# Pooled attention with a SoLU feed-forward: later key loads, transposes on TensorE in its transpose form, and the first tile's scores half by half

## The chip, the cores and the metric

The kernel runs on one core of a Trainium2 chip. A core has TensorE (matrix products into PSUM), VectorE, ScalarE, GpSimd and SyncE, each with an instruction queue of its own; DMAs are issued from the queues of SyncE and ScalarE and share sixteen DMA engines. The metric is the device time of one execution in microseconds (us), as the median of several runs.

## The reference

Two stages in a row. The attention pools `kv` over 4x4 patches (768 keys for each of 4 batches, keys and values the same), and the feed-forward is a SoLU with a layer norm inside:

```python
kv_pool = kv.reshape(B, H // r, r, W // r, r, C).mean(axis=(2, 4))
k = v = kv_pool.reshape(B, -1, C) @ w_sr
s = scale * (q @ k.transpose(0, 2, 1))          # 12288 queries x 768 keys, 4 batches
a = exp(s - s.max(-1)); a /= a.sum(-1) + 1e-09
x = a @ v
h = x @ w_in                                     # 128 -> 1024
solu = h * softmax(h)
ln = (solu - mean) / sqrt(var + 1e-06) * g_ln
out = ln @ w_out                                 # 1024 -> 128
```

All data are float32; the queries are eight times as large as the attention's setup draws them. The output has 49152 rows of 128.

## The kernel before

The 49152 query rows are 384 tiles of 128 rows, four tiles to a group, 96 tiles to a batch. Each product of two float32 operands is made of three products of high and low halves (fp16, or fp32r for the scores of batch 0, where `wide` holds).

One loop runs over slots 0 to 383 (L1081 to L1147). A slot works on several tiles at once, each in another stage: scores and their exponential for tile `slot`, values for an earlier group, h, its exponential and u for tile `slot - 10`, and the output product o for tile `slot - 13`. The order of the calls in the loop is the order of the instructions on every engine, since it is written by hand (`manual_schedule`, L888).

For one tile: `scores_pe` (L580) makes the scores s in PSUM, 128x768, as two halves of 384 columns with three products each; `scores_exp` (L600) takes the maximum on VectorE (nm), the exponential on ScalarE in place and a scaled copy to fp16 (phl, L614); `scores_split` (L617) makes the low half and has SyncE's queue transpose both through a DMA (pT). `values` (L630) accumulates xa on TensorE, `hidden_pe` makes h, `hidden_max`, `hidden_exp` and `hidden_u` make u on VectorE and ScalarE, `hidden_high` and `hidden_low` split u on GpSimd (uhl), `hidden_turn` (L778) transposes it through a DMA on SyncE's queue (uT, four buffers), `hidden_var` (L801) squares u on ScalarE, and `final_pe` (L816) makes o with 24 products of 128 columns.

SyncE's queue holds, per group of four slots, eight of these transposing DMAs, one query load (qf, 256 KB, in the fourth slot) and one output store (out, 256 KB, in the second).

The keys of the next batch are prepared while the current one runs. `kv_plan` (L502) gives each step a slot: sixteen loads of 384 KB (`kv_load`, L226, on ScalarE's queue), additions on GpSimd (`kv_add`), and from slot 70 the steps of `key_steps` (L1039): keys, their squares and halves, and for the batches 1 and 2 the values, in slots 82, 83 and 86 (`kv_vp` on TensorE, `kv_vo` on ScalarE), then their high and low halves on GpSimd. `kv_vp` multiplies two 128x128 blocks of the keys by a diagonal matrix `dg`, which transposes and scales them; it writes to the part of a scores tile in PSUM that the scores leave free. Batch 0's keys are made ahead of the loop, half by half (L941 to L960), with the first two tiles' scores behind them (L1079, L1080). The last tile's u is transposed on TensorE, by a product with the identity (`hidden_turn_pe`, L782), and copied out by ScalarE and VectorE (room).

In the loop the key loads of a slot stand at its end, behind everything else:

```python
        for st in todo:
            if st[0].func is kv_add:
                for f in st:
                    f()
            elif len(st) == 1:
                st[0]()
```

Of the kernel before, what the change touches and what calls it, by code (L numbers as in the profile page):

```python
# [31 lines left out]
GT = 4  # L32
# [29 lines left out]
FIT_AT = 302  # L62

SOON = {0: (), 1: (8, 8), 2: (8, 8), 3: (27, 33), 4: (39, 45), 5: (51, 54)}
LATE = {6: (12, 16, 18), 7: (16, 20, 22)}


@with_exitstack
def kernel(
# [15 lines left out]
    nc = tc.nc  # L85
# [64 lines left out]
    state = {}  # L150
# [133 lines left out]
        nc.vector.tensor_scalar(kq[:, 1:2], kq[:, 2:3], SCALE, None, op0=ALU.mult)  # L284

    def kv_rescale():
        small(state["dg", 0], state["dg", 0], state["kq", 0][:, 2:3])
        nc.gpsimd.tensor_tensor(
            root, state["sv", 0][:, 0:1], state["kq", 0][:, 2:3], op=ALU.mult
        )  # L290
# [51 lines left out]
    def small(dst, src, first, second=1.0):  # L342
        nc.gpsimd.tensor_scalar(dst, src, first, second, op0=ALU.mult, op1=ALU.mult)
# [88 lines left out]
    def in_pairs(name, b, c):  # L432
        return state[name, b][:, c * 256 : c * 256 + 256].rearrange("p (j k) -> p j k", j=2)
# [9 lines left out]

    def kv_vp(b, c):
        for j in range(2):
            nc.tensor.matmul(
                state["free"][:, j, :],
                in_pairs("kT", b, c)[:, j, :],
                state["dg", b],
                start=True,  # L450
                stop=True,
            )

    def kv_vo(b, c):
        nc.scalar.copy(in_pairs("vf", b, c), state["free"])

    def kv_v_high(b, half):
        nc.gpsimd.tensor_scalar(
# [43 lines left out]
    def kv_plan(b):  # L502


        for pos in range(RR):


            if b == 1 and pos in SOON:
                for half, slot in enumerate(SOON[pos]):
                    yield slot, [partial(kv_add, b, half, pos)]  # L510
                continue
            slot = 6 * pos - (28 if b == 1 else 30)
            load, *adds = (slot // GT * GT, slot + 3, slot + 5)
            if b == 1 and pos in LATE:
                load, *adds = LATE[pos]
            yield load, [partial(kv_load, b, pos)]
            if pos:
                for half, add in enumerate(adds):
                    yield add, [partial(kv_add, b, half, pos)]
        for slot, half, *fs in key_steps(b):  # L520
            yield slot, [partial(f, b, half) for f in fs]
# [18 lines left out]
    def wide(g):  # L540
        return g < GPB or g >= NG

    def q_scale(g):
        if wide(g) or NG <= g:
            return
        qf = state["qf", g // QL][:, (g % QL) * 512 : (g % QL + 1) * 512]
        nc.gpsimd.tensor_scalar(
            qf, qf, state["kq", g // GPB][:, 1:2], 1.0, op0=ALU.mult, op1=ALU.mult
        )
# [30 lines left out]
    def scores_pe(t):  # L580
        g, j = divmod(t, GT)
        b = t // TPB
        qh, ql = state["q", g]
        names = ("kwh", "kwl") if wide(g) else ("kh", "kl")
        kh, kl = (state[n, b] for n in names)
        tokens = in_tiles if wide(g) else by_tile
        s = ps_r.tile([P, 2, 512], F32, tag="r", name=f"s_{t}")
        for n, (lh, rh) in enumerate(((qh, kh), (qh, kl), (ql, kh))):
            for half in range(2):
                nc.tensor.matmul(  # L590
                    s[:, half, :384],
                    tokens(lh)[:, j, :],
                    rh[:, half * 384 : (half + 1) * 384],
                    start=n == 0,
                    stop=n == 2,
                )
        state["s", t] = s[:, :, :384]
        state["free"] = s[:, :, 384:]

# [182 lines left out]
    def hidden_turn_pe(t):  # L782

        u, _ = state["u", t]
        pt = ps_r.tile([P, DFF], F32, tag="r", name=f"ut_{t}")
        for c in range(NFC):
            cs = slice(c * P, (c + 1) * P)
            nc.tensor.matmul(pt[:, cs], u[:, cs], ident, start=True, stop=True)
        state["ut", t] = pt.rearrange("p (c d) -> p c d", c=NFC)

    def hidden_turned_high(t):
# [9 lines left out]
    def hidden_var(t):  # L801
        g, j = divmod(t, GT)
        u, su = state.pop(("u", t))

        junk = wrk.tile([P, DFF], BF16, tag="junk", name=f"junk_{t}", bufs=1)
        nc.scalar.activation(  # L806
            junk,
            u,
            AF.Square,
            scale=-float(DFF),  # L810
            bias=su,
            accum_out=state["v3", g][:, j : j + 1],
        )
# [54 lines left out]
    root = fit[:, B - 1 : B]  # L868
    ident = const.tile([P, P], F32, name="ident")
# [39 lines left out]
    for _ in range(WARM):  # L909
# [4 lines left out]
            start=True,  # L914
            stop=True,
# [123 lines left out]
    def key_steps(b):  # L1039
        steps = [  # L1040
            (70, 0, kv_kp, kv_ko), (71, 1, kv_kp, kv_ko), (74, 2, kv_kp, kv_ko),
            (72, 0, kv_sq), (75, 1, kv_sq),
            (77, 0, kv_kh), (79, 1, kv_kh),
            (78, 0, kv_kl), (80, 1, kv_kl),
        ]
        if b < B - 1:
            return steps + [
                (82, 0, kv_vp, kv_vo), (83, 1, kv_vp, kv_vo), (86, 2, kv_vp, kv_vo),
                (84, 0, kv_v_high), (85, 0, kv_v_low), (87, 1, kv_v_high), (88, 1, kv_v_low),
            ]  # L1050
        return steps + [
            (82, 0, kv_v_scale), (84, 1, kv_v_scale),
            (83, 0, kv_vt_high), (86, 1, kv_vt_high),
            (86, 0, kv_vt_low), (88, 1, kv_vt_low),
            (90, 0, kv_v_turn),
        ]
# [3 lines left out]
    def at(t, fn, *args):  # L1060
        if 0 <= t < NT:
            fn(t, *args)

    def at_last(t, fn, *args):

        if 0 <= t < NT and t % GT == GT - 1:
            fn(t // GT, *args)

    def at_soon(t, fn):

        at_last(t, fn) if t >= GT else fn(0) if t == GT - 2 else None
# [9 lines left out]
    for slot in range(NT):  # L1081
        i = slot - LH
        av, qtr = divmod(slot - LAV - GT + 1, GT)
        tb, ti = divmod(slot, TPB)
        if ti == 12 and tb + 1 < B:
            kv_alloc(tb + 1)
        qs = GT if slot < 2 * GT else 2 * GT + 1 if slot < 3 * GT else 3 * GT + QSP
        todo = plan.pop(slot, [])
        at(slot, scores_exp)
        for f in held:  # L1090
            f()
        held = []
        if slot <= LH:
            at(slot - 1, scores_split)
        at(i - 1, hidden_u)
        at_last(slot - XSP - 1, values_split)
        if slot < 9:
            for f in fill.pop(slot, []):
                f()
        if 0 <= av < NG:  # L1100
            values(av, qtr, 0)
        if slot != 8:
            at(slot + 2 if slot < 8 else slot + 1, scores_pe)
        at_soon(slot - NORM, values_norm)
        at_last(slot - FSC, final_scale)
        at(i - 1, hidden_high)
        at(i - 1, hidden_low)
        at_last(slot - FSC, final_root)
        if slot < NT and 0 < qs < slot and (slot - 1 - qs) % GT == 0:
            q_low(slot // GT + 1)  # L1110
        if slot < NT and 0 < qs <= slot + 1 and (slot + 1 - qs) % GT == 0:
            q_scale((slot + 1) // GT + 1)
        if slot < NT - 1:
            at(i - 1, hidden_var)
        at(i, hidden_max)
        at(i, hidden_exp)
        if slot == NT - 1:
            hidden_var(i - 1)
        for f in fill.get(slot, []):
            f()  # L1120
        pairs = [st for st in todo if len(st) > 1 and st[0].func is not kv_add]
        for st in pairs:
            st[0]()
        if 0 <= av < NG:
            values(av, qtr, 1)
        for st in pairs:
            held += st[1:]
        if slot >= LH:
            at(slot, scores_split)
        at_soon(slot - NORM, values_recip)  # L1130
        at_soon(slot - NORM, values_recip_u)
        at(i + 1, hidden_pe)
        if slot < NT - 1:
            at(slot - LO, final_pe)
        at(i - 1, hidden_turn)
        if slot % GT == GT - 1:
            q_load(slot // GT + 3)
        at_last(slot - LO - 1, final_out)
        at_last(slot - XSP, values_out)
        for st in todo:  # L1140
            if st[0].func is kv_add:
                for f in st:
                    f()
            elif len(st) == 1:
                st[0]()
        if slot < NT and 0 < qs <= slot and (slot - qs) % GT == 0:
            q_split(slot // GT + 1)  # L1147
# [144 lines left out]
    n = nc.values_load(count[0:1, 0:1], min_val=0, max_val=P)  # L1292
# [37 lines left out]
```

## Time and profile before

| what | us |
|---|---|
| median of 3 runs | 1836.55 |
| lowest and highest | 1835.77, 1844.36 |
| the profiled execution's own time | 1841.4 |
| its span, first to last instruction | 1839.5 |
| TensorE busy in the span | 1818.2 |
| VectorE, ScalarE, GpSimd busy | 1768.4, 1749.2, 1665.6 |

TensorE's clock was granted at 0.999 of full speed over the span. The busy time of an engine is the time in which it ran an instruction; waiting, branching and the issue of DMAs are not counted. Matmuls are pipelined, so TensorE's busy time has products that overlap. A group of four tiles takes between 18 and 20 us, and nearly all groups look alike, so what a change does is read from the few stretches that differ.

### The profile page before, as it was taken

The numbers are of one execution on the slowest core, as the hardware profiler recorded it, in microseconds if no ns is written. First come the engines' busy times: TensorE is split into PE (matmuls) and PEld (weight loads), VectorE is DVE, ScalarE is ACT, GpSimd is POOL, SyncE is SP. The second block draws the span as 40 slices with busy tenths as digits, with TensorE's granted clock in tenths as the row PEclk, the third lists the DMA queues.
The fourth block names the chain that finished last, engine by engine and source line by source line (L and its number), as shares of the span: only waits on it lengthen the run. The fifth ranks groups of instructions, "written<-read, shape, count | busy, mean of one in ns | idle before, by whom it ended". The sixth has DMA issues, their size and how long they took to land.

```text
span 1839.5 us, 42799 instructions
## 1 busy us (share of the span) xinstructions
PE 1818.2 (99%) x15747; PEld 1216.9 (66%) x15747; DVE 1768.4 (96%) x2635; ACT 1749.2 (95%) x3129; POOL 1665.6 (91%) x1466
## 2 busy tenths in 40 slices
PE   8999999999999999999999999999999999999998
PEld 5577777777666666566666666666666666666666
DVE  6999999999999999999999999999999999999997
ACT  5999999999999999899999999999999999999997
POOL 5899999899999999889999999998988988888887
PEclk9999999999999999999999999999999999999999
DMA  8999999999999999999999999999999999999998
GB/s 301 202 243 241 237 242 242 237 230 231 250 230 250 250 233 234 225 245 235 235 244 249 236 243 248 244 233 221 233 240 231 222 230 229 235 227 236 223 226 170
DMA packets 1440026, 432.79 MB, mean 235 GB/s; under 512 B 1404608, under 2 KB 1408832, under 8 KB 1439552
## 3 DMA queue, kind: packets, MB, share of 16 engines
q1 hardware_dynamic: 1433616, 413.45, 111.3%
q10 hardware_dynamic: 6192, 16.52, 3.5%
q8 instruction: 126, 2.06, 0.5%
q14 instruction: 92, 0.75, 0.1%
HBM read 52.50 MB, written 25.17 MB: 42 GB/s over the span
## 4 chain that ended last, share of the span: by engine, by line
PE 82%; ACT 8%; DVE 3%; DMA 2%; issue 2%; POOL 2%; SPq 0%; DVEq 0%; POOLq 0%; ACTq 0%
PE o L831 24%; PE h L703 23%; PE s L590 18%; PE xa L650 17%; ACT e L727 2%; ACT junk L806 2%; ACT phl L614 2%; ACT s L612 1%; DMA uT<-uhl 1%; DMA kv<-in_kv_dram 1%; POOL uhl L765 1%; DVE junkd L711 1%; DVE nm L611 1%; POOL uhl L758 1%; DVE phl L622 1%
## 5 line engine op out<-in xcount | busy, mean ns | idle before, releaser
L765 POOL TENSOR_TENSOR uhl<-u,uhl 128x1024 f16<-128x1024 f32 x382 | 814.5, 2133 | 31.7
L831 PEld LDWEIGHTS <-uT 128*128 128x128 f16 x9072 | 537.2, 98 | 95.9 <-DMA uT<-uhl 9.6
L831 PE MATMUL o<-wch,uT 128*128 128x128 f16 x6048 | 568.2, 219 | 5.0 <-DMA uT<-uhl 4.8
L831 PE MATMUL o<-wcl,uT 128*128 128x128 f16 x3024 | 526.1, 219 | 0.0
L741 DVE SCALAR_TENSOR_TENSOR u<-h,rz,e 128x1024 f32<-128x1024 f32 x384 | 491.1, 1279 | 26.4 <-ACT e L727 18.9
L711 DVE TENSOR_SCALAR_CACHE_REDUCE junkd<-h,rz 128x1024 bf16<-128x1024 f32 x384 | 490.7, 1278 | 1.5 <-PE h L703 1.1
L758 POOL TENSOR_SCALAR uhl<-u 128x1024 f16<-128x1024 f32 x379 | 395.8, 1044 | 84.7 <-DVE u L741 76.4
L650 PE MATMUL xa<-pT,vhl 128*128 128x512 f16 x1728 | 469.8, 380 | 0.0
L727 ACT ACTIVATE e<-h,nm,rz 128x1024 f32<-128x1024 f32 x384 | 458.5, 1194 | 3.0 <-DVE junkd L711 3.0
L806 ACT ACTIVATE junk<-u,su 128x1024 bf16<-128x1024 f32 x384 | 438.0, 1141 | 0.1
L611 DVE TENSOR_REDUCE nm<-s 128x1 f32<-128x768 f32 x384 | 363.9, 948 | 16.8 <-PE s L590 13.1
L612 ACT ACTIVATE s<-s,nm 128x768 f32<-128x768 f32 x384 | 335.0, 872 | 41.1 <-DVE nm L611 40.9
L622 DVE SCALAR_TENSOR_TENSOR phl<-s,phl 128x768 f16<-128x768 f32 x384 | 365.6, 952 | 2.9 <-ACT phl L614 2.9
L614 ACT ACTIVATE phl<-s 128x768 f16<-128x768 f32 x384 | 311.1, 810 | 12.2
L703 PEld LDWEIGHTS <-xh 128*128 128x128 f16 x1536 | 141.0, 97 | 194.5 <-DVE phl L622 32.3
L650 PEld LDWEIGHTS <-vhl 128*128 128x128 f16 x1728 | 162.5, 98 | 135.5 <-issue 12.8
L703 PE MATMUL h<-w_in_h,xh 128*128 128x512 f16 x768 | 229.1, 380 | 1.6 <-DVE rz L685 1.0
L703 PE MATMUL h<-w_in_h,xl 128*128 128x512 f16 x768 | 228.5, 379 | 0.0
L703 PE MATMUL h<-w_in_l,xh 128*128 128x512 f16 x768 | 228.5, 379 | 0.0
L590 PEld LDWEIGHTS <-qh 128*128 128x128 f16 x1152 | 124.2, 113 | 43.7 <-issue 0.7
L590 PE MATMUL s<-kh,qh 128*128 128x384 f16 x576 | 140.6, 326 | 0.6 <-DVE u L741 0.6
L590 PE MATMUL s<-kh,ql 128*128 128x384 f16 x576 | 140.9, 326 | 0.0
(153 smaller groups left out, 1816.8 us busy)
## 6 DMA issues: line engine op xcount, KB each, us to landing
qf<-in_q_dram SPq DMA_DIRECT2D x96, 256.0 KB, 3.6
out_dram<-ob SPq DMA_DIRECT2D x96, 256.0 KB, 2.7
kv<-in_kv_dram ACTq DMA_DIRECT2D x42, 384.0 KB, 4.4
kv<-in_kv_dram SPq DMA_DIRECT2D x22, 384.0 KB, 7.5
pT<-phl SPq DMA_TRANSPOSE x384, 4.0
uT<-uhl SPq DMA_TRANSPOSE x378, 4.5
raw_in<-in_moe_w_in_dram SPq DMA_DIRECT2D x1, 1024.0 KB, 5.0
raw_out<-in_moe_w_out_dram SPq DMA_DIRECT2D x1, 1024.0 KB, 9.8
```

Source lines behind the costliest of these rows:

```text
L590: nc.tensor.matmul(s[:, half, :384], tokens(lh)[:, j, :], rh[:, half * 384 : (half + 1) * 384], start=n == 0, stop=n == 2,)
L611: nc.vector.tensor_reduce(nm, s, axis=AX.XY, op=ALU.max, negate=True)
L622: nc.vector.scalar_tensor_tensor(phl[:, 1], state.pop(("s", t)), SC, phl[:, 0], op0=ALU.mult, op1=ALU.subtract)
L650: nc.tensor.matmul(xa, v[:, c, :], pT[:, :, a * NKC + c, :], start=n == 0, stop=n == len(seq) - 1)
L703: nc.tensor.matmul(h[:, hs], lh[:, ts], rh[:, hs], start=n == 0, stop=n == 2)
L711: nc.vector.tensor_scalar(junk, state["h", t], state["rz", g][1][:, j : j + 1], None, op0=ALU.mult, op1=ALU.min, accum_out=nm,)
L727: nc.scalar.activation(e, state["h", t], AF.Exp, bias=nm, scale=state["rz", g][0][:, js], accum_out=state["z2", g][:, js],)
L741: nc.vector.scalar_tensor_tensor(u, state.pop(("h", t)), state["rz", g][2][:, j : j + 1], state.pop(("e", t)), op0=ALU.mult, op1=ALU.mult, ...
L758: nc.gpsimd.tensor_scalar(uhl[:, 0, :], u, 1.0, 1.0, op0=ALU.mult, op1=ALU.mult)
L765: low.tensor_tensor(uhl[:, 1, :], u, uhl[:, 0, :], op=ALU.subtract)
L806: nc.scalar.activation(junk, u, AF.Square, scale=-float(DFF), bias=su, accum_out=state["v3", g][:, j : j + 1],)
L831: nc.tensor.matmul(po[:, ts], uT[:, a * NFC + c, :], w[:, c, :], start=start, stop=stop)
```

## The change

Four edits:

- A key load is put into the second slot of a group in place of the first (`slot // GT * GT + 1`, and two entries of LATE by one), and is issued ahead of `hidden_var`, in the middle of the slot, in place of at its end.
- The values of batches 1 and 2 (`kv_vp`) are transposed with `nc.tensor.transpose` and the identity; the scale `root` is applied by ScalarE's eviction (`kv_vo`), and the rescaling of `dg` in slot 17 goes.
- The last tile's u (`hidden_turn_pe`) is transposed with `nc.tensor.transpose` too.
- Tile 0's scores are made first for the one half of the keys, then for the other, the low part of the second half last.

```diff
-LATE = {6: (12, 16, 18), 7: (16, 20, 22)}
+LATE = {6: (13, 16, 18), 7: (17, 20, 22)}
...
     def kv_rescale():
-        small(state["dg", 0], state["dg", 0], state["kq", 0][:, 2:3])
         nc.gpsimd.tensor_tensor(
             root, state["sv", 0][:, 0:1], state["kq", 0][:, 2:3], op=ALU.mult
         )
...
     def kv_vp(b, c):
         for j in range(2):
-            nc.tensor.matmul(
-                state["free"][:, j, :],
-                in_pairs("kT", b, c)[:, j, :],
-                state["dg", b],
-                start=True,
-                stop=True,
-            )
+            nc.tensor.transpose(state["free"][:, j, :], in_pairs("kT", b, c)[:, j, :], ident)
 
     def kv_vo(b, c):
-        nc.scalar.copy(in_pairs("vf", b, c), state["free"])
+        nc.scalar.mul(in_pairs("vf", b, c), state["free"], root)
...
-            load, *adds = (slot // GT * GT, slot + 3, slot + 5)
+            load, *adds = (slot // GT * GT + 1, slot + 3, slot + 5)
...
-        for n, (lh, rh) in enumerate(((qh, kh), (qh, kl), (ql, kh))):
-            for half in range(2):
-                nc.tensor.matmul(
-                    s[:, half, :384],
-                    tokens(lh)[:, j, :],
-                    rh[:, half * 384 : (half + 1) * 384],
-                    start=n == 0,
-                    stop=n == 2,
-                )
+        terms = ((qh, kh), (qh, kl), (ql, kh))
+        order = [(n, half) for n in range(3) for half in range(2)]
+        if t == 0:
+            order = [(0, 0), (1, 0), (2, 0), (0, 1), (2, 1), (1, 1)]
+        for n, half in order:
+            lh, rh = terms[n]
+            nc.tensor.matmul(
+                s[:, half, :384],
+                tokens(lh)[:, j, :],
+                rh[:, half * 384 : (half + 1) * 384],
+                start=n == 0,
+                stop=(n, half) in order[4:] if t else (n, half) in (order[2], order[5]),
+            )
...
-            nc.tensor.matmul(pt[:, cs], u[:, cs], ident, start=True, stop=True)
+            nc.tensor.transpose(pt[:, cs], u[:, cs], ident)
...
+        for st in todo:
+            if st[0].func is kv_load:
+                st[0]()
         if slot < NT - 1:
             at(i - 1, hidden_var)
...
-            elif len(st) == 1:
+            elif len(st) == 1 and st[0].func is not kv_load:
                 st[0]()
```

ScalarE's queue around the load of one sixteenth of batch 1's keys (kv_12), before: xh is the eviction of xa in a group's first slot, s and phl are the exponential and the scaled copy of the second slot's tile, junk the square of u, e the exponential of h.

```order
L806 ACTIVATE junk_2964,v_8_2764<-u_2950,su_2951 128x1024
L727 ACTIVATE e_2969,z_8_2763<-h_2909,nm_34_2966,rz_2741 128x1024
L657 ACTIVATE xh_3010<-xa_2754,sv_115 128x512
L230 DMA kv_12_3013<-in_kv_dram 128x768
L612 ACTIVATE s_2954,z_all<-s_2954,nm_3015 128x2x384
L614 ACTIVATE phl_3018<-s_2954 128x768
L806 ACTIVATE junk_3038,v_8_2764<-u_3020,su_3021 128x1024
L727 ACTIVATE e_3043,z_8_2763<-h_2977,nm_35_3040,rz_2741 128x1024
```

And in the changed kernel, whose lines stand three further up in this part:

```order
L803 ACTIVATE junk_2963,v_8_2763<-u_2949,su_2950 128x1024
L724 ACTIVATE e_2968,z_8_2762<-h_2908,nm_34_2965,rz_2740 128x1024
L654 ACTIVATE xh_3009<-xa_2753,sv_115 128x512
L609 ACTIVATE s_2953,z_all<-s_2953,nm_3012 128x2x384
L611 ACTIVATE phl_3015<-s_2953 128x768
L230 DMA kv_12_3035<-in_kv_dram 128x768
L803 ACTIVATE junk_3037,v_8_2763<-u_3017,su_3018 128x1024
L724 ACTIVATE e_3042,z_8_2762<-h_2976,nm_35_3039,rz_2740 128x1024
```

The load has moved behind the second slot's exponential and scaled copy; nothing else on this queue has moved.

TensorE's queue at the first two tiles' scores (s_281 and s_288; kwh and kwl are the high and low parts of the keys, qwh and qwl of the queries), before:

```order
L202 MATMUL pk_1_257<-kv_6_154,w_sr_93 128x384
L590 MATMUL s_281<-kwh_119,qwh_235 128x384 x2
L590 MATMUL s_281<-kwl_120,qwh_235 128x384 x2
L590 MATMUL s_281<-kwh_119,qwl_236 128x384 x2
L590 MATMUL s_288<-kwh_119,qwh_235 128x384 x2
L590 MATMUL s_288<-kwl_120,qwh_235 128x384 x2
```

And in the changed kernel:

```order
L202 MATMUL pk_1_257<-kv_6_154,w_sr_93 128x384
L587 MATMUL s_281<-kwh_119,qwh_235 128x384
L587 MATMUL s_281<-kwl_120,qwh_235 128x384
L587 MATMUL s_281<-kwh_119,qwl_236 128x384
L587 MATMUL s_281<-kwh_119,qwh_235 128x384
L587 MATMUL s_281<-kwh_119,qwl_236 128x384
L587 MATMUL s_281<-kwl_120,qwh_235 128x384
L587 MATMUL s_288<-kwh_119,qwh_235 128x384 x2
L587 MATMUL s_288<-kwl_120,qwh_235 128x384 x2
```

The first half's three products now stand ahead of the second half's, and the product with the low part of the second half's keys is the last of the six; tile 1 is as it was. On TensorE the value steps and the last u keep their places, and only their operand is another; the order on VectorE and SyncE is the same as before, and GpSimd has one instruction less.

## Rows read from the trace of the kernel before

**Rows 1.** The page, part 1: engine, busy us (share of the span), instructions.

```profile
PE 1818.2 (99%) x15747; PEld 1216.9 (66%) x15747; DVE 1768.4 (96%) x2635; ACT 1749.2 (95%) x3129; POOL 1665.6 (91%) x1466
```

**Rows 2.** Waits of TensorE, whole span: what waits, for what; total us, count, longest.

```profile
PE o L831 <- DMA uT<-uhl: 4.8, 5, 2.1
```

**Rows 3.** Windows: us, PE, PEld, DVE, ACT, POOL busy, clock, DMA, GB/s.

```profile
735.84:781.84 46.00, 42.15 (x368) 27.26 (x367) 41.46 (x62) 40.97 (x75) 40.62 (x37) 1.00 1.19 225
```

**Rows 4.** Waits of TensorE, 725 to 775 us.

```profile
PE o L831 <- DMA uT<-uhl: 3.9, 3, 2.1
```

**Rows 5.** The chain: start, us, what; the chain's step at 739.40 us.

```profile
739.40 8.21 DMA uT<-uhl
```

**Rows 6.** Timeline of ScalarE's queue, the same place: start, us, line, operation.

```profile
740.23 0.34 ACTq L230 DMA_DIRECT2D kv<-in_kv_dram  x1
```

**Rows 7.** Timeline of ScalarE, 575 to 596 us, a quiet group.

```profile
592.91 0.33 ACTq L230 DMA_DIRECT2D kv<-in_kv_dram  x1
...
594.54 0.81 ACT L614 ACTIVATE phl<-s 128x768 f16<-128x768 f32 x1
```

**Rows 8.** Timeline of SyncE's queue, 575 to 596 us.

```profile
593.83 0.58 SPq L531 DMA_DIRECT2D qf<-in_q_dram  x1
...
595.91 3.11 SPq L780 DMA_TRANSPOSE uT<-uhl  x1
```

**Rows 9.** Line 780's DMAs, 1100 to 1200 us, then 1400 to 1500 us.

```profile
DMA to landing us min/median/max: 3.8/5.0/8.5
...
DMA to landing us min/median/max: 3.7/4.2/5.5
```

**Rows 10.** Groups by line: xcount | busy us, mean ns | idle before.

```profile
L442 ACT ACTIVATE kT<-s,kq 128x256 f32<-128x256 f32 x9 | 4.2, 468 | 0.0
...
L446 PE MATMUL s<-dg,kT 128*128 128x128 f32 x24 | 3.6, 275 | 0.0
...
L455 ACT COPY vf<-s 128x256 f32<-128x256 f32 x6 | 2.2, 367 | 0.0
...
L343 POOL TENSOR_SCALAR dg<-dg,kq 128x128 f32<-128x128 f32 x1 | 0.4, 362 | 0.0
```

**Rows 11.** The chain: the same product in two groups of tiles each.

```profile
91.31 1.34 PE o L831 x24
...
110.04 1.34 PE o L831 x24
...
392.88 1.34 PE o L831 x24
...
412.46 1.34 PE o L831 x24
```

**Rows 12.** Windows around two value groups, columns as above.

```profile
844.00:863.00 19.00, 19.00 (x170) 13.01 (x169) 18.03 (x28) 18.15 (x35) 18.34 (x18) 1.00 1.15 238
...
882.00:901.00 19.00, 18.45 (x163) 11.96 (x161) 18.77 (x29) 18.19 (x33) 18.24 (x17) 1.00 1.19 239
```

**Rows 13.** The chain at the first tile's scores.

```profile
28.37 1.40 PE s L590 x5
...
30.78 1.00 ACT s L612 x2
```

**Rows 14.** Timeline of VectorE, 18 to 50 us.

```profile
28.35 0.56 DVE L214 SCALAR_TENSOR_TENSOR kwl<-pk,kwh 128x384 fp32r<-128x384 f32 x1 [4.10 <-ACT kwh L211]
```

**Rows 15.** The chain at the program's end.

```profile
1824.37 2.02 PE ut L788 x16
...
1826.40 6.74 PE o L831 x120
```

**Rows 16.** Line 780's last DMAs: those under way at 1826.1 to 1826.4 us.

```profile
L780 SPq DMA_TRANSPOSE room<-uhl x2: 1902/2519/3136, 1824.2 to 1826.2; - x2
...
DMA to landing us min/median/max: 5.2/5.4/5.6
```

**Rows 17.** Windows at the program's end, columns as above.

```profile
1824.00:1834.00 10.00, 8.88 (x140) 8.59 (x137) 5.20 (x10) 7.24 (x13) 4.03 (x7) 1.00 0.99 206
```

## The prediction

> **What bounds the kernel now.** I read four views, each narrower than the one before it. The page's first part gives TensorE busy for 99% of the span [rows 1]. The other engines follow closely, so the time that the change can give back lies in three places: TensorE's idle time, instructions on TensorE itself, and the head and tail of the program. The view of waits, for TensorE alone, tells of the first: its longest entry is the product o (L831) waiting for the transposed u that SyncE's DMA queue brings (uT): 4.8 us in five waits [rows 2]. The table of windows shows that this is no steady loss: in the window from 735.84 us TensorE is busy for 42.15 of 46 us [rows 3], and the waits of 725 to 775 us are 3.9 us of the 4.8, three waits, so 1.3 us each [rows 4]. The chain of waits says how one begins: the transposition of u issued at 739.40 needs 8.21 us to land [rows 5], and ScalarE's queue issued a key load 0.83 us behind it, at 740.23 [rows 6].
>
> **The sum's base.** The rows come from an execution of 1841.4 us (1839.5 us of span and 1.9 around it). The median run, 1836.55, is 4.85 us shorter, the fastest, 1835.77, 5.6. That is the size of the 4.8 us of uT waits. So my estimate is that a median run has next to none of them; I make the sum against 1841.4 and compare it with the median.
>
> **Part 1, the key loads.** 42 loads move on ScalarE's queue past two instructions, the exponential of the scores (L612) and the scaled copy (L614). In a quiet group the load goes out at 592.91 and the scaled copy starts at 594.54 [rows 7]. The queue issues while the engine works, so the load would go out at about 594.6, 1.7 us later. On SyncE's queue the query load (L531) goes out at 593.83 and the next transposition of u at 595.91 [rows 8]. So the load falls behind the query load, where it was 0.9 us ahead of it, and comes 1.3 us ahead of that transposition, where it was 3.0. At the bad place it would go out at about 741.9, 2.5 us behind the transposition issued at 739.40.
> Issuing takes ScalarE's queue 0.33 us per load [rows 7], 13.9 us in all. It was hidden under the eviction of xa and the wait for the maximum; it will be hidden under the scaled copy. Behind it stands the square of u (L806), then the exponential of h, whose result VectorE waits for; if the cover fails, up to 13.9 us come on top. I take nothing.
> The transfers themselves are neither fewer nor smaller. In a stretch with loads (1100 to 1200 us) a transposition of u lands in 5.0 us at the median and 8.5 at most, in one without (1400 to 1500) in 4.2 and 5.5 [rows 9]. So the presence of a load costs up to 3.0 us of landing; what its place is worth lies between losing all five waits (-4.8) and new ones (priced under the rivals). I take -4.8 for the profiled execution: its worst waits begin with a load 0.8 us behind a transposition, and this goes. For a median run the same is 0. No load is late for its addition: the nearest addition stands two slots behind the load's new place, some 9 us.
>
> **Part 2, values through the transpose form.** Six steps, three for each of two batches, of two products each. Now they are 24 records of 128 columns in fp32 [rows 10], that is four to a step. The transposition at the end runs 16 such records in 2.02 us [rows 15], 0.126 each, so a step takes 0.50. This shows in the pace: a group of four tiles takes 110.04 - 91.31 = 18.73 us, the one with two of the steps 412.46 - 392.88 = 19.58 [rows 11], 0.85 more.
> No row shows the new form. Nearest from below: a 128-column product in fp16 takes 1.34 / 24 = 0.056 [rows 11], two of them 0.11, which saves 0.39 a step and 2.3 us in all. From above: records of 275 ns [rows 10] that do not overlap, four to a step, 1.10, a loss of 0.60 a step and 3.6 us. I take one fp32 record in place of two, 0.25 a step: 1.5 us off TensorE, being nearest to the row of the operation that it replaces.
> What is late next? ScalarE's eviction becomes a scaling one, 468 in place of 367 ns [rows 10], and GpSimd makes the high and low halves of the values in the same slots: in the windows 844 to 863 and 882 to 901 it is busy for 18.34 and 18.24 of 19 us, with no rest but the gaps between its instructions, and in the later one TensorE idles, 18.45 of 19 [rows 12]. Time that TensorE gains there it will mostly wait for GpSimd later. I keep a third: -0.5 us. The removed GpSimd scaling (dg, 0.36 us [rows 10]) comes once, far from these slots, where GpSimd's backlog empties: 0, at most -0.36.
>
> **Part 3, the first tile.** Now the second half's high product waits for its key half until 28.37, and the first tile's scores end at 28.37 + 1.40 = 29.77; ScalarE's first exponential follows at 30.78 [rows 13]. The last input, the low part of the second key half, is ready at 28.35 + 0.56 = 28.91 [rows 14]. In the new order three products of the first half run in the wait, and behind 28.91 one product stands where three did. Five records and the wait took 1.40; one takes some 0.3 to 0.4 to its end. So the scores end at about 29.3, -0.45; ScalarE runs without a break from there, so I take -0.4 (0 if another input of the first slots takes its place).
>
> **Part 4, the last u.** The transposition takes 2.02 us, and the 120 products behind it 6.74, to 1833.14 [rows 15]. Halved, it frees 1.0 us. But the last of those products need a transposed u that is issued at 1826.2 and lands 5.2 us later, at 1831.4 [rows 16]; their 24 records begin at 1833.14 - 6.74 / 5 = 1831.79. So no more than 0.4 can come out: -0.3. If the new records do not overlap, 16 of 275 ns [rows 10], 4.4 us, it is +2.4.
>
> **Sum.** 1841.4 - 4.8 - 0.5 - 0.4 - 0.3 = 1835.4. From the median, without the 4.8: 1836.55 - 1.2 = 1835.35. The forecast is 1835.4.
>
> **The rivals.**
> Everything gained stays: the new form at its cheapest and GpSimd not in the way, 2.3 + 0.45 + 0.4 = 3.2 us from 1836.6: 1833.4. For it: TensorE is the busiest engine and idles little. Against it: GpSimd's windows.
> The waits only move: a load delays whichever transpositions are in flight, and the five waits come at other places: 1841.4 - 1.2 = 1840.2. For it: the transfers are the same. Against it: the quiet groups have a load too and no wait.
> The Trainium skill speaks for this rival: "DMA: Bandwidth & Descriptors", Queues, rings and completion order, says that each DMA engine takes turns between the queues with work, so a load on a second queue slows the transpositions wherever it stands. The landing times [rows 9] agree with that as far as they go; they favour no place.
> Slower: the load now stands 1.3 us ahead of the second slot's transposition in every group, and what happened at 739.40 (8.2 us to land) happens there. Each such wait costs 1.3 us [rows 4]. From eight of the 42 loads on, 10.4 us, it is slower by over 0.5%; at twelve, 15.6 us, 1851.0. For it: the distance of load and transposition gets shorter, and 8.2 us came at a distance of 0.8. Against it: there the load was behind the transposition with the query load behind both.
> The clock falls at the end: behind the eight transpositions of the last u TensorE's granted clock is 1.2 GHz in place of 2.4, and the 6.74 us of products behind them [rows 15] double: 1835.4 + 6.7 = 1842.1. Now the clock is granted in full (1.00) over them [rows 17]. Against it: the transpositions are short and products stand on both sides.
> The Trainium skill names this: "TensorE: Matmul & The Clock Gate", Part 4: PE-mode transpose, says that a product in transpose mode does not count as busy for the clock gate in the same way. No row here has that mode, so the trace can't say.
>
> **Chances.** Forecast 0.54, all stays 0.16, waits move 0.14, clock 0.05, slower 0.07; 0.04 for a gain that I see no row for. What a measurement can tell from no change is about 0.5%, 9.2 us, so 1827.4 to 1845.7 is no change: 0.54 + 0.16 + 0.14 + 0.05 = 0.89; slower 0.07, faster 0.04. The range goes from 1831.5 (all stays, and 1.9 us for a session that runs a little faster) to 1842.5, which takes in the moved waits and the clock; it leaves out the slower case and the unexplained gain.
>
> **What would show it.** In the profile after: TensorE's waits for uT below 2 us with no window of 46 us under 45; the loads' issue behind the query load's; 12 records of a transposition in the value steps in place of 24, and the group with two steps at about 19.1 to 19.3 us; TensorE's wait before the second half of tile 0 shorter and the first exponential at about 30.35; the u transposition at about 1.0 us, with the last products then waiting for a DMA. It is wrong if uT waits gather in the second slot, if GpSimd shows rest in the value groups (then more stays), or if the clock row at the end is under 1.00.

## The result, and the profile after

The changed kernel takes 1866.53 us at the median of six runs (1858.72 to 1884.2); the kernel before, with three more runs beside it, 1840.75 (1835.77 to 1844.36). The ratio is 1.0137 (95% interval 1.0097 to 1.0178): slower, where no change was forecast, and outside the range. The profiled execution took 1868.9 us, 27.5 more than the one before.

The page's first lines, changed kernel (they answer [rows 1]):

```profile
span 1867.0 us, 42757 instructions
...
PE 1824.0 (98%) x15727; PEld 1216.6 (65%) x15727; DVE 1770.6 (95%) x2635; ACT 1753.5 (94%) x3129; POOL 1667.9 (89%) x1465
```

TensorE idles for 1867.0 - 1824.0 = 43.0 us, where it was 1839.5 - 1818.2 = 21.3. So 21.7 us of the 27.5 are idle time of TensorE. The other 5.8 are busy time of the same work; most of it is a lower clock behind the longest waits, shown below.

Which stretch lost it: windows of the changed kernel with loads (60 to 1330 us) and behind them, then the same of the kernel before; columns are us and busy time by engine, clock, DMA share and GB/s.

```profile
60.00:1330.00 1270.00, 1241.03 (x10745) 833.71 (x10745) 1208.97 (x1794) 1206.87 (x2156) 1161.92 (x1011) 1.00 1.19 233
1330.00:1800.00 470.00, 469.86 (x4135) 307.98 (x4134) 462.87 (x691) 454.68 (x819) 416.38 (x367) 1.00 1.16 231
```

```profile
60.00:1330.00 1270.00, 1262.24 (x10999) 851.22 (x11000) 1234.21 (x1835) 1229.67 (x2205) 1186.45 (x1036) 1.00 1.18 238
1330.00:1800.00 470.00, 469.99 (x4134) 307.65 (x4133) 462.88 (x691) 453.40 (x817) 413.30 (x366) 1.00 1.16 230
```

With loads TensorE idles for 29.0 us, before for 7.8: 21.2 more. Without loads both lose nothing. What it waits for there is in the view of waits, changed kernel (total us, times, longest; it answers [rows 2]):

```profile
PE o L828 <- DMA uT<-uhl: 26.6, 24, 5.0
```

That is 21.8 us more than the 4.8 of before, the whole of the added idle time. Behind the three longest of these waits (2.48, 5.05 and 2.82 us, ending at 79.30, 123.61 and 887.36 us) TensorE's granted clock falls to 1.2 GHz, half of full speed. Windows of the changed kernel, columns as above:

```profile
79.40:82.80 3.40, 3.40 (x27) 3.31 (x27) 0.26 (x1) 1.78 (x4) 2.73 (x3) 0.50 1.20 243
123.70:127.10 3.40, 3.40 (x27) 3.31 (x28) 0.00 (x0) 0.41 (x2) 2.39 (x4) 0.51 1.39 169
888.30:891.70 3.40, 3.40 (x19) 1.97 (x17) 0.06 (x1) 0.22 (x2) 3.32 (x5) 0.50 1.21 298
```

TensorE is busy throughout, at half its speed: 1.7 us lost in each, 5.1 of the 5.8 us, as an estimate. The kernel before has no such stretch in its loop. So a long wait is paid twice, as idle time and in the clock behind it.

The landing times of the transpositions of u (from the issue until the data has arrived) show why TensorE waits: first the changed kernel's line 777, then line 780 of the kernel before, both from 60 to 1330 us.

```profile
DMA to landing us min/median/max: 3.7/4.8/12.2
```

```profile
DMA to landing us min/median/max: 3.6/4.8/8.9
```

The median stays; the longest grow. The longest of all, in the chain of waits of the changed kernel (start, us, what):

```profile
111.33 12.24 DMA uT<-uhl
...
123.61 1.49 PE o L828 x13
```

SyncE's and ScalarE's queues ahead of it, in the timeline (start, us in the queue):

```profile
108.60 0.57 SPq L524 DMA_DIRECT2D qf<-in_q_dram  x1
109.28 1.96 SPq L622 DMA_TRANSPOSE pT<-phl  x1
111.33 8.69 SPq L777 DMA_TRANSPOSE uT<-uhl  x1
```

```profile
109.52 0.34 ACTq L230 DMA_DIRECT2D kv<-in_kv_dram  x1
```

The key load goes out 1.8 us ahead of the transposition, 0.9 behind the query load: the order that the prediction expected in all groups, and the one of 31 of the 42. (In program order the transposition that is hit stands in the first slot; SyncE's queue runs behind ScalarE's.) What the DMA engines do meanwhile, in the DMA view of 111.3 to 117.4 us, changed kernel; q1 is SyncE's queue, q10 ScalarE's, with packets, MB and share of 16 engines:

```profile
DMA packets 1388, 0.62 MB, mean 102 GB/s; under 512 B 1291, under 2 KB 1291, under 8 KB 1388
...
q1 hardware_dynamic: 1280, 0.32, 74.4%
q10 hardware_dynamic: 108, 0.30, 44.6%
```

And of before, 595.9 to 602.0 us, where the load is all but through when the transposition is issued at 595.91 [rows 8]:

```profile
DMA packets 5424, 1.63 MB, mean 267 GB/s; under 512 B 5278, under 2 KB 5278, under 8 KB 5424
...
q1 hardware_dynamic: 5390, 1.57, 114.3%
q10 hardware_dynamic: 34, 0.06, 2.4%
```

The engines are as busy in both (the shares of both queues add up to 119 and 117%), but here, with both queues at work, they move 102 GB/s in place of 267. This is the worst case: around three other late transpositions of the changed kernel the same view gives 145 GB/s (69.5 to 79.2 us), 153 (876.5 to 887.3) and 220 (839.0 to 846.8), and around the one at 739.40 of the kernel before 187.

### The profile page after: what moved, and what is told of

Same layout as the page of the kernel before. It is cut to its first block, busy times and chain, and to the rows that moved or that the text cites. A ratio compares the mean times of both kernels' runs of the same rounds, so it can differ in the third digit from the quotient of the medians.

```text
span 1867.0 us, 42757 instructions
## 1 busy us (share of the span) xinstructions
PE 1824.0 (98%) x15727; PEld 1216.6 (65%) x15727; DVE 1770.6 (95%) x2635; ACT 1753.5 (94%) x3129; POOL 1667.9 (89%) x1465
## 4 chain that ended last, share of the span: by engine, by line
PE 39%; ACT 18%; DVE 16%; DMA 10%; issue 9%; POOL 7%; SPq 0%; DVEq 0%; POOLq 0%; ACTq 0%
PE o L828 12%; PE h L700 10%; PE s L587 9%; DMA uT<-uhl 9%; PE xa L647 8%; ACT e L724 5%; ACT junk L803 5%; DVE junkd L708 4%; DVE nm L608 4%; ACT phl L611 4%; DVE phl L619 3%; POOL uhl L762 3%; ACT s L609 2%; POOL uhl L755 2%; DVE u L738 2%
## 5 line engine op out<-in xcount | busy, mean ns | idle before, releaser
L828 PE MATMUL o<-wch,uT 128*128 128x128 f16 x6048 | 571.1, 220 | 27.0 <-DMA uT<-uhl 26.6
L587 PE MATMUL s<-kl,qh 128*128 128x384 f16 x576 | 141.0, 327 | 0.0
```

The source lines that it names most:

```text
L587: nc.tensor.matmul(s[:, half, :384], tokens(lh)[:, j, :], rh[:, half * 384 : (half + 1) * 384], start=n == 0, stop=(n, half) in order[4:] ...
L828: nc.tensor.matmul(po[:, ts], uT[:, a * NFC + c, :], w[:, c, :], start=start, stop=stop)
```

## The experiments

Theory A: the load's new place delays the transposition of u that comes next. Rival B: one of the other three edits costs the time. C: the load does harm only right behind the query load. D: a load costs the same wherever it is. E: two queues at once are what stretches both. Each ratio is to runs of the kernel before on the same chip; "waits" are those of TensorE's product o for uT in the profiled run. The edits are shown by their main lines; "..." marks lines left out.

| run | load | median us | ratio (95%) | waits us |
|---|---|---|---|---|
| e1 | old place, other edits on | 1844.4 | 1.0022 (0.9993 to 1.0052) | 1.9 |
| e2 | new place, other edits off | 1868.09 | 1.0149 (1.0122 to 1.0175) | 22.0 |
| e3 | a slot later | 1848.23 | 1.0040 (1.0020 to 1.0060) | 14.8 |
| e4 | new place, query load later | 1894.38 | 1.0298 (1.0236 to 1.0360) | 40.6 |
| e5 | ahead of xa's eviction | 1857.58 | 1.0084 (1.0055 to 1.0114) | 14.9 |
| e6 | behind the exponential of h | 1874.56 | 1.0152 (1.0104 to 1.0200) | 38.8 |
| e7 | halves, old place | 1838.57 | 0.9981 (0.9955 to 1.0007) | 2.1 |
| e8 | SyncE's queue, ahead of uT | 1862.12 | 1.0099 (1.0064 to 1.0134) | 22.5 |
| e9 | halves, new place | 1845.33 | 1.0023 (1.0005 to 1.0041) | 12.2 |
| e10 | halves, old place, other edits off | 1840.2 | 0.9993 (0.9977 to 1.0008) | 3.1 |
| e11 | quarters, from the old place on | 1838.92 | 0.9988 (0.9971 to 1.0004) | 9.2 |
| e12 | SyncE's queue, behind uT | 1848.8 | 1.0041 (1.0025 to 1.0057) | 11.2 |

### Which edit

e1 undoes the load's move alone, e2 makes it alone:

```diff
-LATE = {6: (13, 16, 18), 7: (17, 20, 22)}
+LATE = {6: (12, 16, 18), 7: (16, 20, 22)}
...
-            load, *adds = (slot // GT * GT + 1, slot + 3, slot + 5)
+            load, *adds = (slot // GT * GT, slot + 3, slot + 5)
...
-        for st in todo:
-            if st[0].func is kv_load:
-                st[0]()
         if slot < NT - 1:
             at(i - 1, hidden_var)
...
-            elif len(st) == 1 and st[0].func is not kv_load:
+            elif len(st) == 1:
```

> The changed kernel with the key loads back at the end of a group's first slot; the other three edits stay. Theory A (the load's new place delays the second slot's transposition of u): the long waits for uT go, TensorE's two rows of waits for uT fall from 70 us to 10 to 16 us, and the time is 1834 to 1841 us, 1 to 2 us under the kernel before. Theory B (the transpose form or the new order of tile 0 costs the time): it stays at 1858 to 1884 us. Theory C (the load does harm only because it now stands right behind the query load): as A.

> The kernel before with the key loads alone moved to the middle of the second slot. Theory A: 1858 to 1884 us, 20 to 70 us of waits of TensorE for uT. Theory B: 1835 to 1844 us. Theory C: as A.

The waits of TensorE, e1, then e2:

```profile
PE o L828 <- DMA uT<-uhl: 1.9, 3, 0.9
```

```profile
PE o L831 <- DMA uT<-uhl: 22.0, 16, 3.9
```

B falls on both sides: the move alone makes all of the loss (1.0149 beside 1.0137). e1 comes out no faster than before, 3 us above the top of A's range. The stretches at 1.2 GHz go with the waits: in the profiled runs, from 60 us to the end of the loop, there are three in e2 and e4, four in e6, two each in e3, e5 and e8, and none in e1, e7 and e9 to e12.

### The query load, and another slot

e3 moves the load one slot on; e4 leaves it and has the query load two slots later:

```diff
-            load, *adds = (slot // GT * GT + 1, slot + 3, slot + 5)
+            load, *adds = (slot // GT * GT + 2, slot + 3, slot + 5)
...
-        if slot % GT == GT - 1:
-            q_load(slot // GT + 3)
+        if slot % GT == 1 and slot >= GT:
+            q_load(slot // GT + 2)
```

> The changed kernel with the loads one slot later, in the middle of the third slot: as near ahead of a transposition of u as now (1 to 2 us), but 4 to 5 us behind the query load. Theory A: the waits move to the third slot's transposition, and the time stays at 1855 to 1880 us. Theory C: no pair of loads, so 1834 to 1844 us.

> The changed kernel with the query load two slots later (some 9 us), the key load where the change put it. Theory A: the key load still stands 1 to 2 us ahead of the second slot's transposition, 1855 to 1885 us. Theory C: 1834 to 1844 us, with that transposition landing in 4 to 6 us.

C as the only cause falls: e4 parts the two loads and is the slowest of all, above A's range too. Its query load now stands near the output store, ahead of another transposition, so there are two places to wait (40 waits). e3 lies between A's numbers and C's: 18 waits, longest 2.2 us, so the slot with the query load in it is the dearer place. Whether the query load or the smaller room for that transposition makes it so, the times don't part. The landings say that a key load is enough: with one 0 to 2 us ahead and the query load over 6 us away, 20 transpositions of u in e4 land in 7.2 us at the median and 10.9 at most; with a query load 0 to 4 us ahead and no key load within 4, 38 in e3 land in 4.5 and 6.4.

### Earlier, later

e5 and e6 start from the changed kernel and put the load earlier (first slot, ahead of xh) and later (second slot, behind the exponential of h):

```diff
-            load, *adds = (slot // GT * GT + 1, slot + 3, slot + 5)
+            load, *adds = (slot // GT * GT, slot + 3, slot + 5)
...
         at(i, hidden_exp)
+        for st in todo:
+            if st[0].func is kv_load:
+                st[0]()
```

(e6 has the second piece alone; in both the piece ahead of `hidden_var` goes.)

> The changed kernel with the loads ahead of the eviction of xa in the first slot, some 0.8 us earlier than in the kernel before, so 3.5 us ahead of the transposition of u that comes next and 1.2 us behind the last one. Theory A (what counts is how long the load has been on its way when a transposition is issued: 1 to 2 us ahead is worst): the next transposition lands in 5.5 us in place of 6.5 to 7, the one before it in 5.5 to 6, waits for uT under 10 us, 1833 to 1840 us. Rival D (the load costs the same wherever it stands, its bytes count): 1840 us or more with the same sum of waits as the kernel with the loads put back.

> The changed kernel with the loads behind the exponential of h, 2.5 us later than the change puts them, so about 1 us behind the transposition of u that was hit. Theory A: that transposition is already on its way and lands in 5.5 to 7.5 us in place of 7 to 12, and the time falls to 1840 to 1855 us. Rival D: 1858 to 1884 us as the changed kernel.

Both miss A's numbers. In e5's trace the load goes out 0.6 us ahead of the transposition before at the median, not 1.2 behind it: it no longer stands behind the eviction's wait, and met another transposition. TensorE's product xa waits there too, 13.3 us in all, 4.8 of them for pT; in the kernel before it doesn't wait. In e6 the load goes out 0.1 us behind the transposition at the median, which did not help: landings reach 10.9 us. So A's form "a load 1 to 2 us ahead is worst" was too narrow, and D falls as well, since the places differ by 1.5%.

What fits is read from single transpositions, not from the medians of a version. Here are all transpositions of u that start between 60 and 1330 us in the eight versions with whole loads on ScalarE's queue (before, changed, e1 to e6), by when the nearest key load goes out:

| the load goes out | transpositions | landing, median us | longest us |
|---|---|---|---|
| 2 to 3 us ahead | 66 | 6.3 | 8.4 |
| 1 to 2 us ahead | 92 | 7.3 | 12.2 |
| 0 to 1 us ahead | 76 | 7.2 | 10.8 |
| 0 to 1 us behind | 55 | 7.6 | 10.9 |
| 1 to 2 us behind | 75 | 5.8 | 8.0 |
| 2 to 4 us behind | 182 | 4.1 | 7.3 |
| over 4 us away on either side | 1540 | 4.5 | 7.7 |

So a load does harm from about 3 us ahead to about 2 us behind, and most from 2 ahead to 1 behind. The distance alone doesn't give the time of a version: in e3 33 transpositions have a load between 2 us ahead and 1 us behind, in the changed kernel 27, and e3 is the faster one. Whether a late landing makes TensorE wait hangs also on the room that each slot leaves it, which was not measured.

### The size of one load

e7 issues each load as two DMAs of 192 KB, at the old place and two slots later; e9 the same from the new place; e10 is e7 without the other edits; e11 has four of 96 KB in four slots. The edit of e7 and e9; e11's does the same with quarters and four slots in a row:

```diff
-            yield load, [partial(kv_load, b, pos)]
+            yield load, [partial(kv_load, b, pos, 0)]
+            yield load + 2, [partial(kv_load, b, pos, 1)]
...
+            eng.dma_start(t[:, half, :], src[:, half, :])
```

> The changed kernel with each key load as two DMAs of 192 KB, one where the kernel before has the load, one two slots later. If the size of one load beside a transposition counts (theory A in this form): a transposition lands in at most 6.5 us, waits for uT are under 5 us in all, 1832 to 1838 us. If the bytes count wherever they are (D): 1838 to 1846 us, the waits spread over two slots.

> The changed kernel with each key load as two DMAs of 192 KB, the first where the change puts the load, the second two slots later, also in the middle of a slot. If the size of what stands ahead of a transposition counts: the second slot's landings stay under 7.5 us and the time is 1836 to 1846 us, like the halves at the old place. If the place alone counts: twice as many transpositions are hit, 1855 to 1890 us.

> The kernel before with the loads in halves as at the old place, and none of the change's edits. It shows what the other three edits are worth where few waits for uT disturb: with the halves and those three edits the time was 1838.57 us. If they give the 1.2 us of the prediction: 1839.8 us; if nothing: 1838.6; if they cost: under 1838.

> The changed kernel with each key load as four DMAs of 96 KB, one at the end of each of four slots. If the size of one load beside a transposition counts: no transposition lands later than 6.5 us and TensorE waits for uT under 2 us in all, 1834 to 1837 us. If the bytes count wherever they are: 1836 to 1846 us, no better than halves.

Landing of the transpositions of u in e9, 60 to 1330 us, beside 12.2 us at most with whole loads:

```profile
DMA to landing us min/median/max: 3.7/4.9/8.3
```

At the new place halves take away 1.1% of the 1.4%, with the same bytes and twice as many loads: the size of one load beside a transposition counts. The hit transposition still lands in up to 8.3 us where under 7.5 was expected. At the old place halves and quarters are not told from the kernel before, and quarters are no better than halves (9.2 us of waits where under 2 were expected). Their longest landings, 7.9 us in e7 and 8.2 in e11, are over the 6.5 expected as well. e7 is the lowest median of all, but its interval holds 1; no version is shown to beat the kernel before.

### One queue

e8 issues the load from SyncE's queue right ahead of the transposition that was hit, e12 right behind it (both with the load in the first slot; the last piece shown is e8's, in e12 it stands behind `hidden_turn`):

```diff
-    def kv_load(b, pos, eng=nc.scalar):
+    def kv_load(b, pos, eng=nc.sync):
...
+        for st in todo:
+            if st[0].func is kv_load:
+                st[0]()
         at(i - 1, hidden_turn)
```

> The changed kernel with the key loads on SyncE's queue, right ahead of the transposition of u that was hit, so that load and transposition are issued one after the other from one queue. Rival E (two queues working at once is what stretches both): the transposition lands in under 7 us and the time is 1834 to 1848 us. Theory A (a load just ahead of the transposition delays it, whatever the queue): its landing stays at 7 us or more, TensorE waits for uT over 30 us, 1855 to 1885 us.

> The changed kernel with the key loads on SyncE's queue, right behind the transposition of u that was hit, in place of right ahead of it. Theory A (a load just ahead of a transposition delays it): that transposition lands in 4 to 5 us as without a load; the next one starts some 4 us behind the load and lands in under 6; 1834 to 1845 us. If any load on SyncE's queue costs: 1855 to 1865 us as right ahead.

Landings in e8, 60 to 1330 us, then e12:

```profile
DMA to landing us min/median/max: 3.7/4.8/7.9
```

```profile
DMA to landing us min/median/max: 3.6/4.5/7.1
```

E explains the tail and not the whole. On one queue no transposition takes over 7.9 us (12.2 in the changed kernel and 10.9 in e6, on two), and a load lands in 6.4 at most (10.9 in the changed kernel). The DMA engines keep 201 and 209 GB/s around two of e8's loads (301.1 to 308.3 and 187.9 to 194.9 us). But a load 0.7 us ahead on the same queue still makes 25 waits, 22.5 us where A had over 30, and the time stays A's. Behind the transposition e12 gives back more than half of that: 1848.8, still above A's range.

## Why the prediction was wrong

**The base** isn't borne out. The three runs shown were a low draw; six gave a median of 1840.75, near the profiled run's 1841.4. That a median run has next to none of the waits was read off that draw: e1's profiled run has 1.9 us of them in place of 4.8, and takes 1839.97 us.

**Part 1 failed**, at the step "I take -4.8 for the profiled execution: its worst waits begin with a load 0.8 us behind a transposition, and this goes". The geometry was right in kind (behind the query load, ahead of the transposition by 1.3; 1.8 in the rows above), but one quiet group stood for all: over the 42 loads the medians go from 2.6 us ahead of that transposition to 1.6, and from 0.2 us behind the query load to 0.8. The sign was not right: that nearness does harm from the front as from behind. Measured is +21.8 us of waits where -4.8 was taken, and the clock's 5.1, for which the sum had no term. The 8.2 us of [rows 5] showed what a load near a transposition costs; I read it as a matter of which goes first, though [rows 7] and [rows 8] showed the gap shrinking. ScalarE's queue did hide the issue, as taken: VectorE's wait for the exponential did not grow (before, then changed):

```profile
DVE u L741 <- ACT e L727: 18.9, 89, 0.5
```

```profile
DVE u L738 <- ACT e L724: 15.4, 70, 0.5
```

**The slower rival** named mechanism, place and threshold. From eight waits of 1.3 us it was to be slower; there were 24 of 1.1 us (26.6 / 24), or 1.3 with the clock's 5.1. It had 0.07. The argument against it, that at 739.40 the load was behind the transposition, is what e6 and the changed kernel refute together.

**The rival "the waits only move"** (1840.2) falls: the load's place is worth 1.4% here. The Trainium skill's rule beside it, that each DMA engine takes turns between the queues with work ("DMA: Bandwidth & Descriptors", Queues, rings and completion order), I had read as "no place is better". Two queues did stretch each other, which agrees with the rule (12.2 us to land, 7.9 at most in e8). That the total rate falls, to 102 GB/s at worst, does not follow from turns alone; what costs it inside the DMA engines stays open.

**Part 2** was right in its rows, answering [rows 10, 11]; lines of the changed kernel, then its chain:

```profile
L445 PE MATMUL s<-ident,kT 128*128 128x128 f32 x12 | 2.3, 272 | 0.0
...
L448 ACT ACTIVATE vf<-s,fit 128x256 f32<-128x256 f32 x6 | 2.8, 468 | 0.0
```

```profile
404.17 1.34 PE o L828 x24
...
423.31 1.34 PE o L828 x24
```

One record in place of two, the eviction at 468 ns, and the group with two steps at 423.31 - 404.17 = 19.14 us (expected 19.1 to 19.3, before 19.58). What the three edits are worth in the whole isn't settled: e7 and e10, with and without the three edits, give 0.9981 and 0.9993 with overlapping intervals.

**Part 3**: the chain of the changed kernel at the first tile, answering [rows 13]:

```profile
28.18 1.05 PE s L587 x3
...
30.24 1.00 ACT s L609 x2
```

The scores end at 29.23 (expected 29.3), the exponential starts 0.54 us sooner (expected 0.4).

**Part 4**: the last u on TensorE and VectorE's last two steps, changed kernel, then VectorE's of before:

```profile
1852.03 1.06 PE L785 MATMUL ut<-ident,u 128*128 128x128 f32 x8 [0.24 <-DVE u L738]
```

```profile
1850.59 1.28 DVE L738 SCALAR_TENSOR_TENSOR u<-h,rz,e 128x1024 f32<-128x1024 f32 x1 [0.29 <-ACT e L724]
...
1860.83 0.75 DVE L851 SCALAR_TENSOR_TENSOR ob<-o,swi,f 128x512 f32<-128x512 f32 x1 [3.97 <-PE o L828]
```

```profile
1822.93 1.28 DVE L741 SCALAR_TENSOR_TENSOR u<-h,rz,e 128x1024 f32<-128x1024 f32 x1 [0.29 <-ACT e L727]
...
1833.21 0.75 DVE L854 SCALAR_TENSOR_TENSOR ob<-o,swi,f 128x512 f32<-128x512 f32 x1 [3.79 <-PE o L831]
```

The transposition takes 1.06 us, half of 2.02, as taken; from the last u to the last output it is 10.24 us in place of 10.28. So 0.04 comes out where I took 0.3: the last products now wait for their DMA, as the view of waits of the changed kernel has it, which the step had named as its bound. Behind it the last 24 products take 1.53 us, where the step had counted 6.74 / 5 = 1.35.

```profile
PE o L828 <- DMA room<-uhl: 0.6, 2, 0.4
```

The clock rival falls with the window at the end, granted in full behind the transpositions; the clock did fall, but behind the waits of part 1:

```profile
1844.00:1860.00 16.00, 15.20 (x227) 13.41 (x225) 11.55 (x19) 14.60 (x24) 11.40 (x11) 1.00 1.15 236
```

## What to carry to other kernels

Where a transposing DMA lands just in time, read from the trace how far other transfers start from it, on every queue, in all groups and not in one, and price a move by the gap it leaves on both sides, not by which goes first. A large load beside it costs much less in pieces some slots apart (1.0023 in place of 1.0137). A wait that comes in a few groups of before is a sample of what a change makes frequent: multiply it by the number of groups that get the same geometry, and look at the granted clock behind the longest of them.

## What the hardware showed

Two queues at work together, a plain load and a transposition, brought the DMA engines at worst from 267 to 102 GB/s at the same busy share, and held the transposition in SyncE's queue for 8.69 us, which had taken 3.11 [rows 8]; other such stretches had 145 to 220 GB/s. With the same load on SyncE's own queue no landing was over 7.9 us. A load that started from 2 us ahead of a transposition to 1 us behind it brought its median landing from 4.5 to over 7 us. Behind waits of TensorE of 2.48, 2.82 and 5.05 us the granted clock was 0.50 of full speed (1.2 GHz) for 3.4 us each time.
